# Attention tiles of the third and fourth unit: transposed in 32x32 blocks by VectorE and put in place through DRAM, in place of TensorE transposes

## The chip, the cores and the metric

The kernel runs on one core of a Trainium2 chip. The metric is the device time of one execution in microseconds, from repeated executions. A profiled execution leaves a trace, whose span goes from its first to its last instruction. Engines are named as in the profile: PE is TensorE's matmul, PEld its weight load, DVE VectorE, ACT ScalarE, POOL GpSimd and SP SyncE, whose queue issues nearly all DMAs. An L with a number is a line of the kernel.

## What is computed

Chunked attention (batch 8, 8 heads, 576 positions in chunks of 64, head dimension 64), and then a layer of three weight matrices with an elementwise maximum, and a projection:

```python
scores = scale * np.matmul(q_c, k_c.transpose(0, 1, 2, 4, 3))     # 64 x 64 for each chunk and head
scores = scores - np.max(scores, axis=-1, keepdims=True)
attn = np.exp(scores)
attn = attn / (np.sum(attn, axis=-1, keepdims=True) + 1e-09)
out = np.matmul(attn, v_c)
x = out of all heads side by side                                  # 4608 tokens x 512
h = np.maximum(np.maximum(x @ w1, x @ w2), x @ w3)                 # 512 -> 768
result = h @ w_out                                                 # 768 -> 512
```

All is float32. A product of the second part is made from three matmuls (`three`, L184 to L187) on a high and a low part of each operand.

## The kernel before

**Tiles, groups, units.** The 4608 tokens are 36 tiles of 128. Tiles 0 to 7 form the first group, written out by hand (`FIRST`), and a second group. The other 28 are worked in four units of 6, 8, 8 and 6 tiles (`UNITS`, L27). A unit has a hidden stage (9 sets of weights, `hidden`, L481, 14 steps of three matmuls in each set) and then a projection stage (`project`, L565, 6 steps of three matmuls for each tile, all on PE). The weights of a set come from DRAM into a ring of two buffers by two DMAs on SP's queue, of 768 KB (L465) and 1024 KB (L469). The load of set n + 2 is issued when set n is done (L778), and the load of a unit's last but one set takes the next unit's first set.

**Attention of a unit runs inside the hidden stage of the unit before it**, in pairs of tiles: `insertion` (L716) plans the steps of one pair. Pairs 0 to 2 are the first unit's, 3 to 6 the second's, 7 to 10 the third's and 11 to 13 the fourth's. For each tile of a pair: S (scores on PE, 32 small matmuls, L235), mx, sub, exp, sum, eps, rec (DVE and ACT), nrm (POOL, L202: the tile `e` is multiplied by 1 / sum), T (four PE transposes of 128x128 from `e` into PSUM, L258), at (ACT copies them into `xs`, L263), and V (32 small matmuls on PE, L274) in the *next* pair's insertion, with `xs` as the moving operand. V's results are copied into `stage` (L712), from which the next unit's operands are made (`operands`, L456) right behind the hidden stage.

**The order of the work** is fixed when the program is built. A clock `now` runs forward by `STEP_H` (0.6815 for a unit of 8 tiles) for each step of a set, and each planned piece of work has a due time on it. When a step passes it, the piece is emitted into its engine's queue, and `now` moves on by the PE time it is planned with: 0.65 for S, 0.5 for V, 0.46 for T, and nothing for others. All queues work in the order of emission. In a pair planned at `when`, V of the pair before and S come at `when`, and the other steps at `when` + 1 + the number in `PAIR` or `PAIR_T`, the first number for the pair's first tile, the second for its second. Insertions of a series stand at 9.0 behind the unit's start, and then evenly up to the length planned for the hidden stage less 3.5 (L737 to L744), so every 28.9 in the third unit's attention and every 41.6 in the fourth's. The last one of a series scores the next unit's first pair, and its T comes 14 later (`behind`).

**Room.** PSUM holds five banks for the hidden stage, taken in the order in which they came free (`take`, `give`); V takes two of them. Each of `raw`/`kk` (q and k), `vs` (v) and `e`/`et` has one buffer for the even and one for the odd tile; `xs` has two.

```python
def transposed():                                   # L261
    st["at"] = xs_p.tile([P, 4, P], F32, name="xs")
    nc.scalar.copy(out=st["at"], in_=st["tp"])
```

Of the kernel before, what the change touches and what calls it, by code (L numbers as in the profile page):

```python
# [9 lines left out]
F32 = mybir.dt.float32  # L10
# [10 lines left out]
P = 128  # L21
# [10 lines left out]
PAIR = (("mx", 1.4, 2.9), ("sub", 2.2, 3.7), ("exp", 3.1, 4.6), ("sum", 4.1, 6.0), ("eps", 5.0, 6.9), ("rec", 5.2, 7.1),  # L32
        ("nrm", 5.6, 7.5))
PAIR_T = (("T", 10.0, 12.4, 0.46), ("at", 10.9, 13.3, 0.0))
OPERANDS, SLOWER = (0.3, 2.0), (1.0, 1.8)
MIX = 0.5

# [26 lines left out]
def chunk_attn_maxout_kernel(  # L64
# [10 lines left out]
    nc = tc.nc  # L75
# [6 lines left out]
    xs_p = ctx.enter_context(tc.tile_pool(name="xs_p", bufs=2))  # L82
    ep = ctx.enter_context(tc.tile_pool(name="ep", bufs=1))
    ao_p = ctx.enter_context(tc.tile_pool(name="ao_p", bufs=1))
    stage_p = ctx.enter_context(tc.tile_pool(name="stage_p", bufs=1))
    dram = ctx.enter_context(tc.tile_pool(name="dram", bufs=1, space=bass.MemoryType.DRAM))
# [38 lines left out]
    for name in FIRST.split():  # L125
        k = (3 * int(name[1]) + int(name[2])) if name[0] in "WAXY" else None
# [62 lines left out]
    def over_sum(e):  # L189
        sm = tmp.tile([P, 32], F32, name="sm")[:, :8]  # L190

        def total():
            nc.vector.tensor_reduce(out=sm, in_=e, axis=AX.X, op=ALU.add)  # L193

        def guard():
            nc.vector.tensor_scalar_add(sm, sm, 1e-9)  # L196

        def invert():
            nc.vector.reciprocal(out=sm, in_=sm)  # L199

        def norm(eng=nc.gpsimd):
            eng.tensor_tensor(out=e, in0=e, in1=sm.unsqueeze(2).broadcast_to([P, 8, 64]), op=ALU.mult)  # L202

        return total, guard, invert, norm

    halves_of = [slice(0, 64), slice(64, 128)]
# [3 lines left out]
    def bank_of(name):  # L210
        if name not in banks_of:
            banks_of[name] = ps[name].tile([P, 2, 2, 4, 64], F32, name=name[-1])
        return banks_of[name]

    def plain_steps(t, x_of, col):


        st = {}

        def load_qk():  # L220
            st["r"] = att.tile([P, 2, 8, 64], F32, name="buf", tag=("raw", "kk", "aa")[t % 3] if t < 8 else ("raw", "kk")[t % 2],
                               bufs=1)
            nc.sync.dma_start(out=st["r"], in_=qk[t])

        def load_v():
            st["v"] = att.tile([P, 8, 64], F32, name="buf", tag=f"vs{t % 2}", bufs=1)
            nc.sync.dma_start(out=st["v"], in_=vb[t])

        def scores():
            r = st["r"]  # L230
            st["s"] = s = bank_of("ps_s")[:, :, t % 2 if t < 4 or "pair" in st else 0]
            for g in range(4):
                for h, c in quarters:
                    a, b = halves_of[c], halves_of[h]
                    nc.tensor.matmul(out=s[b, c, g, :], lhsT=r[a, 0, 2 * g + h, :], rhs=r[a, 1, 2 * g + h, :],  # L235
                                     start=True, stop=True)

        def maximum():
            st["mx"] = tmp.tile([P, 32], F32, name="mx")[:, :8]
            nc.vector.tensor_reduce(out=st["mx"].rearrange("p (g c) -> p c g", c=2), in_=st["s"], axis=AX.X, op=ALU.max)  # L240

        def less():
            st["e"] = ep.tile([P, 4, 2, 64], F32, name="e", tag=("et", "e")[t % 2])
            most = st["mx"].rearrange("p (g c) -> p c g", c=2)
            nc.vector.tensor_tensor(out=st["e"].rearrange("p g c k -> p c g k"), in0=st["s"],  # L245
                                    in1=most.unsqueeze(3).broadcast_to([P, 2, 4, 64]), op=ALU.subtract)

        def exp():
            nc.scalar.activation(out=st["e"], in_=st["e"], func=AF.Exp, scale=SCALE)

        def total():
            total, st["guard"], st["invert"], st["norm"] = over_sum(st["e"].rearrange("p g c k -> p (g c) k"))
            total()

        def transpose():
            st["tp"] = tp = ps_t.tile([P, 4, P], F32, name="tp")
            for g in range(4):
                nc.tensor.transpose(out=tp[:, g, :], in_=st["e"][:, g].rearrange("p c k -> p (c k)"),  # L258
                                    identity=ident)

        def transposed():  # L261
            st["at"] = xs_p.tile([P, 4, P], F32, name="xs")
            nc.scalar.copy(out=st["at"], in_=st["tp"])  # L263

        def values():
            if "pair" in st:
                x = [p[:, t % 2] for p in st["pair"]["x"]]
            else:
                st["x"] = bank_of("ps_x")[:, :, t % 2] if t < 4 else bank_of("ps_s")[:, :, 1]
                x = [st["x"][:, c] for c in range(2)]  # L270
            for g in range(4):
                for h, c in quarters:
                    a, b = halves_of[c], halves_of[h]
                    nc.tensor.matmul(out=x[c][b, g, :], lhsT=st["v"][a, 2 * g + h, :], rhs=st["at"][a, g, b],  # L274
                                     start=True, stop=True)

        def part(x):
            return x[:, :, col:col + P].rearrange("p g (c x) -> p c g x", c=2)

        def high():  # L280
            nc.scalar.copy(out=part(x_of()[0]), in_=st["x"])

        def low():
            xh, xl = x_of()
            nc.vector.tensor_tensor(out=part(xl), in0=st["x"], in1=part(xh).bitcast(F32), op=ALU.subtract)  # L285

        def pair(both):
            st["pair"] = both

        return dict(q=load_qk, v=load_v, pair=pair, S=scores, mx=maximum, sub=less, exp=exp, sum=total,  # L290
                    eps=lambda: st["guard"](), rec=lambda: st["invert"](), nrm=lambda *eng: st["norm"](*eng),
                    T=transpose, at=transposed, V=values, xh=high, xl=low)

    begun = {}

# [284 lines left out]
    def x_tiles(i):  # L580
        if i not in halves:
            halves[i] = [xp.tile([P, CT, 512], F32R, name=n, tag=f"{n}{i % 2}") for n in ("xh", "xl")]
        return halves[i]
# [22 lines left out]
    for t in range(8):  # L606
        ops.update((f"{n}{t}", fn) for n, fn in plain_steps(t, lambda i=t // 4: x_tiles(i), t % 4 * P).items())
# [57 lines left out]
    def plan(at, pe, fn):  # L665
        heapq.heappush(due, (at, len(order), pe, fn))
        order.append(fn)
# [20 lines left out]
    g = moe(starts[1], lambda: x_tiles(1))  # L688
# [5 lines left out]
    pairs = []  # L694
    for u, (_, t0, count) in enumerate(units):
        for n in range(0, count, 2):
            both = dict(col=n * P, norm=nc.gpsimd if u else nc.vector)
            both["tiles"] = [begun[t] if t in begun else plain_steps(t, stage, (t - t0) * P) for t in (t0 + n, t0 + n + 1)]
            for steps in both["tiles"]:
                steps["pair"](both)  # L700
            pairs.append(both)

    def value_banks(both):
        def fn():
            both["banks"] = [take() for _ in range(2)]
            both["x"] = [p.rearrange("p (s g x) -> p s g x", s=2, g=4) for p, _ in both["banks"]]
        return fn

    def staged(both, c):
        def fn():  # L710
            to = stage()[:, :, both["col"]:both["col"] + 2 * P].rearrange("p g (s c x) -> p c s g x", s=2, c=2)
            nc.scalar.copy(out=to[:, c], in_=both["x"][c])  # L712
            give(both["banks"][c][1])
        return fn

    def insertion(when, k, behind=0.0):  # L716

        scored = pairs[k]["tiles"] if k < len(pairs) else []
        if k:
            plan(when, 0.0, value_banks(pairs[k - 1]))  # L720
            for n, steps in enumerate(pairs[k - 1]["tiles"]):
                plan(when + 0.001 * (n + 1), 0.5, steps["V"])
                plan(when + 1.2 + 0.6 * n, 0.0, staged(pairs[k - 1], n))
        lead = 1.0 * bool(k)
        for n, steps in enumerate(scored):
            plan(when + 0.003 + 0.001 * n, 0.65, steps["S"])
            for name, *at in PAIR:
                fn = steps[name]
                plan(when + lead + at[n], 0.0, (lambda fn=fn: fn(pairs[k]["norm"])) if name == "nrm" else fn)
            for name, *at, pe in PAIR_T:  # L730
                plan(when + lead + behind + at[n], pe, steps[name])
            plan(when + 6.0 + n, 0.0, steps["v"])
        if k + 1 < len(pairs):
            for n, steps in enumerate(pairs[k + 1]["tiles"]):
                plan(when + 4.0 + n, 0.0, steps["q"])
# [99 lines left out]
```

## Time and profile before

| | us |
|---|---|
| median of 3 runs (lowest, highest) | 630.55 (630.23, 631.14) |
| the profiled execution | 631.41 |
| its span, first to last instruction | 629.6 |
| PE busy in it | 619.9 (98%) |
| PEld busy | 529.9 (84%) |
| DVE busy | 415.3 (66%) |
| ACT busy | 233.5 (37%) |
| POOL busy | 218.4 (35%) |
| mean granted TensorE clock | 0.999 of full speed |
| moved by DMA | 133.70 MB, 212 GB/s over the span |

Busy times of PE overlap with one another, as matmuls are pipelined, so 98% says that PE hardly ever stands still, and not how near it is to its peak. The chain of work that ended last gives each piece only the time by which it moves the end, and so tells what a piece on PE costs.

### The profile page before, as it was taken

The numbers are of one execution on the slowest core, as the hardware profiler recorded it, in microseconds if no ns is written. First come the engines' busy times: TensorE is split into PE (matmuls) and PEld (weight loads), VectorE is DVE, ScalarE is ACT, GpSimd is POOL, SyncE is SP. The second block draws the span as 40 slices with busy tenths as digits, with TensorE's granted clock in tenths as the row PEclk, the third lists the DMA queues.
The fourth block names the chain that finished last, engine by engine and source line by source line (L and its number), as shares of the span: only waits on it lengthen the run. The fifth ranks groups of instructions, "written<-read, shape, count | busy, mean of one in ns | idle before, by whom it ended". The sixth has DMA issues, their size and how long they took to land.

```text
span 629.6 us, 12374 instructions
## 1 busy us (share of the span) xinstructions
PE 619.9 (98%) x5102; PEld 529.9 (84%) x5102; DVE 415.3 (66%) x661; ACT 233.5 (37%) x400; POOL 218.4 (35%) x186
## 2 busy tenths in 40 slices
PE   7899999999999999999999999999999999999997
PEld 3788878887899999888888888888888888999986
DVE  4898965777949776956767679346585760366530
ACT  4897644444433242542323325222223141122121
POOL 2422576785413323424242325114141330222210
PEclk9999999999999999999999999999999999999999
DMA  8988658664958773825565717235545061366502
GB/s 329 353 306 264 239 184 326 259 238 162 366 190 299 283 285 140 332 102 218 194 260 184 268 56 312 84 126 226 217 168 209 32 279 67 135 241 256 205 18 83
DMA packets 36055, 133.70 MB, mean 212 GB/s; under 512 B 4000, under 2 KB 6560, under 8 KB 30240
## 3 DMA queue, kind: packets, MB, share of 16 engines
q1 hardware_dynamic: 35856, 132.79, 56.4%
q8 instruction: 40, 0.66, 0.4%
q10 hardware_dynamic: 144, 0.13, 0.1%
q14 instruction: 15, 0.12, 0.1%
HBM read 106.95 MB, written 25.95 MB: 211 GB/s over the span
## 4 chain that ended last, share of the span: by engine, by line
PE 92%; DVE 6%; ACT 1%; issue 1%; POOL 0%; DVEq 0%; ACTq 0%; POOLq 0%
PE pm L185 28%; PE pm L186 28%; PE pm L187 28%; PE s L235 2%; PE pm L274 2%; PE tp L258 2%; PE pm L627 1%; DVE e L245 1%; DVE s L406 1%; DVE sm L193 1%; DVE mx L240 1%; DVE sm L196 0%; POOL c L398 0%; DVE m L329 0%; DVE xl L285 0%
## 5 line engine op out<-in xcount | busy, mean ns | idle before, releaser
L185 PE MATMUL pm<-X,ring 128*128 128x512 f32 (+1 forms) x504 | 185.2, 368 | 0.1
L187 PE MATMUL pm<-X,ring 128*128 128x512 f32 (+1 forms) x504 | 182.5, 362 | 0.0
L186 PE MATMUL pm<-X,ring 128*128 128x512 f32 (+1 forms) x504 | 182.5, 362 | 0.0
L508 POOL TENSOR_TENSOR kept<-kept 128x384 f32<-128x384 f32 (+1 forms) x36 | 41.4, 1151 | 226.4 <-DVE kept L502 217.2
L502 DVE TENSOR_TENSOR kept<-pm,kept 128x384 f32<-128x384 f32 (+1 forms) x72 | 44.7, 621 | 98.4 <-PE pm L187 97.8
L185 PEld LDWEIGHTS pm<-X,ring 128*128 128x128 f32 x504 | 94.6, 188 | 10.7 <-DVE H L524 0.4
L187 PEld LDWEIGHTS pm<-X,ring 128*128 128x128 f32 x504 | 94.6, 188 | 10.1
L186 PEld LDWEIGHTS pm<-X,ring 128*128 128x128 f32 x504 | 94.7, 188 | 9.4
L499 ACT COPY kept<-pm 128x384 f32<-128x384 f32 (+1 forms) x72 | 38.4, 533 | 129.1 <-PE pm L187 124.6
L185 PE MATMUL pm<-woh,H 128*128 128x512 f32 x168 | 66.0, 393 | 0.0
L187 PE MATMUL pm<-woh,H 128*128 128x512 f32 x168 | 65.5, 390 | 0.0
L186 PE MATMUL pm<-wol,H 128*128 128x512 f32 x168 | 65.4, 390 | 0.0
L202 POOL TENSOR_TENSOR e<-e,sm 128x512 f32<-128x512 f32 x27 | 32.2, 1194 | 80.4 <-DVE sm L199 49.5
L185 PE MATMUL pm<-xh,wl 128*128 128x512 f32 (+1 forms) x156 | 60.1, 385 | 0.0
L186 PE MATMUL pm<-xl,wh 128*128 128x512 f32 (+1 forms) x156 | 58.4, 374 | 0.3 <-DVE xl L285 0.3
L187 PE MATMUL pm<-xh,wh 128*128 128x512 f32 (+1 forms) x156 | 58.3, 374 | 0.0
L505 DVE TENSOR_TENSOR pm<-pm,kept 128x384 f32<-128x384 f32 (+1 forms) x72 | 45.3, 629 | 14.8 <-PE pm L187 14.1
L514 DVE TENSOR_TENSOR most<-pm,most 128x384 f32<-128x384 f32 (+1 forms) x72 | 44.8, 622 | 2.1
L520 ACT CAST H<-most 128x384 fp32r<-128x384 f32 (+1 forms) x48 | 26.8, 570 | 43.0 <-DVE most L514 43.0
L240 DVE TENSOR_REDUCE mx<-s 128x8 f32<-128x512 f32 x36 | 24.6, 683 | 20.1 <-PE s L235 20.1
L187 PEld LDWEIGHTS pm<-woh,H 128*128 128x128 f32 x168 | 31.5, 188 | 6.6
L185 PEld LDWEIGHTS pm<-woh,H 128*128 128x128 f32 x168 | 31.5, 188 | 6.4
(93 smaller groups left out, 947.6 us busy)
## 6 DMA issues: line engine op xcount, KB each, us to landing
ring<-w SPq DMA_DIRECT2D x36, 1024.0 KB, 6.8
ring<-w SPq DMA_DIRECT2D x36, 768.0 KB, 4.5
buf<-in_qk SPq DMA_DIRECT2D x36, 512.0 KB, 6.2
buf<-in_vb SPq DMA_DIRECT2D x36, 256.0 KB, 6.5
w<-s SPq DMA_DIRECT2D x9, 1024.0 KB, 4.5
out_x<-ao SPq DMA_DIRECT2D x35, 256.0 KB, 2.0
stage<-in_w SPq DMA_DIRECT2D x7, 512.0 KB, 5.2
xl<-in_w SPq DMA_DIRECT2D x5, 512.0 KB, 8.2
```

The source lines that it names most:

```text
L185: nc.tensor.matmul(out=o, lhsT=al, rhs=bh, start=first, stop=False)
L186: nc.tensor.matmul(out=o, lhsT=ah, rhs=bl, start=False, stop=False)
L187: nc.tensor.matmul(out=o, lhsT=ah, rhs=bh, start=False, stop=last)
L202: eng.tensor_tensor(out=e, in0=e, in1=sm.unsqueeze(2).broadcast_to([P, 8, 64]), op=ALU.mult)
L235: nc.tensor.matmul(out=s[b, c, g, :], lhsT=r[a, 0, 2 * g + h, :], rhs=r[a, 1, 2 * g + h, :], start=True, stop=True)
L240: nc.vector.tensor_reduce(out=st["mx"].rearrange("p (g c) -> p c g", c=2), in_=st["s"], axis=AX.X, op=ALU.max)
L499: return lambda: nc.scalar.copy(out=kept(k), in_=o[i])
L502: return lambda: nc.vector.tensor_tensor(out=kept(k), in0=o[i], in1=kept(q), op=plus)
L505: return lambda: nc.vector.tensor_tensor(out=o[i] if w else M(j, c), in0=o[i], in1=kept(k), op=plus)
L508: nc.gpsimd.tensor_tensor(out=kept(2), in0=kept(2), in1=kept(1), op=plus)
L514: return lambda: nc.vector.tensor_tensor(out=M(j, c), in0=of(), in1=M(j, c), op=most)
L520: nc.scalar.copy(out=hh[j][:, c * half:(c + 1) * half], in_=M(j, c))
```

## The change

In the pairs of the third and fourth unit (pairs 7 to 13, 14 tiles; `u > 1`) T and at are replaced by three steps. `bt`: DVE transposes the tile's 32x32 blocks, in two instructions of 128x256, into a buffer of `xs`. `bw`: one DMA on SP's queue writes that tile (256 KB, in pieces of 1 KB) to DRAM. `br`: two DMAs on SP's queue read it back (128 KB each, in pieces of 512 bytes, 64 partitions each) into a new tile in the buffer of `e`, so that each block stands where the whole transpose would have it. V then takes its moving operand of 64 columns as two runs of 32. `now` is not moved forward for the new steps. Due times against `when`: bt at 9.6 and 11.5, bw at 10.6 and 12.5, br at 15.6 and 16.6 (T was at 11.0 and 13.4, at at 11.9 and 14.3).

```diff
--- before.py
+++ after.py
@@ -32,6 +32,7 @@
 PAIR = (("mx", 1.4, 2.9), ("sub", 2.2, 3.7), ("exp", 3.1, 4.6), ("sum", 4.1, 6.0), ("eps", 5.0, 6.9), ("rec", 5.2, 7.1),
         ("nrm", 5.6, 7.5))
 PAIR_T = (("T", 10.0, 12.4, 0.46), ("at", 10.9, 13.3, 0.0))
+PAIR_D = (("bt", 8.6, 10.5, 0.0), ("bw", 9.6, 11.5, 0.0), ("br", 14.6, 15.6, 0.0))
 OPERANDS, SLOWER = (0.3, 2.0), (1.0, 1.8)
 MIX = 0.5
 
@@ -262,6 +263,26 @@
             st["at"] = xs_p.tile([P, 4, P], F32, name="xs")
             nc.scalar.copy(out=st["at"], in_=st["tp"])
 
+        def blocks():
+            st["b"] = xs_p.tile([P, 4, 4, 32], F32, name="xs")
+            for c in range(2):
+                nc.vector.transpose(out=st["b"][:, 2 * c:2 * c + 2], in_=st["e"][:, :, c].rearrange("p g (k two) -> p two g k", two=2))
+
+        def to_scratch():
+            st["d"] = dram.tile([2, P, 2 * P], F32, name=f"b{t}")
+            nc.sync.dma_start(out=st["d"].rearrange("c p x -> p c x"), in_=st["b"].rearrange("p (c j) g x -> p c (j g x)", c=2))
+
+        def from_scratch():
+            st["at"] = ep.tile([P, 4, 4, 32], F32, name="e", tag=("et", "e")[t % 2])
+            for c, rows in enumerate(halves_of):
+                nc.sync.dma_start(out=st["at"][rows].rearrange("p i g x -> p i (g x)"),
+                                  in_=st["d"][c].rearrange("(i k) (j x) -> (k j) i x", i=4, j=2))
+
+        def moving(a, g, b):
+            if "d" in st:
+                return st["at"][a, b.start // 32:b.stop // 32, g, :]
+            return st["at"][a, g, b]
+
         def values():
             if "pair" in st:
                 x = [p[:, t % 2] for p in st["pair"]["x"]]
@@ -271,7 +292,7 @@
             for g in range(4):
                 for h, c in quarters:
                     a, b = halves_of[c], halves_of[h]
-                    nc.tensor.matmul(out=x[c][b, g, :], lhsT=st["v"][a, 2 * g + h, :], rhs=st["at"][a, g, b],
+                    nc.tensor.matmul(out=x[c][b, g, :], lhsT=st["v"][a, 2 * g + h, :], rhs=moving(a, g, b),
                                      start=True, stop=True)
 
         def part(x):
@@ -289,7 +310,7 @@
 
         return dict(q=load_qk, v=load_v, pair=pair, S=scores, mx=maximum, sub=less, exp=exp, sum=total,
                     eps=lambda: st["guard"](), rec=lambda: st["invert"](), nrm=lambda *eng: st["norm"](*eng),
-                    T=transpose, at=transposed, V=values, xh=high, xl=low)
+                    T=transpose, at=transposed, bt=blocks, bw=to_scratch, br=from_scratch, V=values, xh=high, xl=low)
 
     begun = {}
 
@@ -694,7 +715,7 @@
     pairs = []
     for u, (_, t0, count) in enumerate(units):
         for n in range(0, count, 2):
-            both = dict(col=n * P, norm=nc.gpsimd if u else nc.vector)
+            both = dict(col=n * P, norm=nc.gpsimd if u else nc.vector, turn=PAIR_D if u > 1 else PAIR_T)
             both["tiles"] = [begun[t] if t in begun else plain_steps(t, stage, (t - t0) * P) for t in (t0 + n, t0 + n + 1)]
             for steps in both["tiles"]:
                 steps["pair"](both)
@@ -727,7 +748,7 @@
             for name, *at in PAIR:
                 fn = steps[name]
                 plan(when + lead + at[n], 0.0, (lambda fn=fn: fn(pairs[k]["norm"])) if name == "nrm" else fn)
-            for name, *at, pe in PAIR_T:
+            for name, *at, pe in pairs[k]["turn"]:
                 plan(when + lead + behind + at[n], pe, steps[name])
             plan(when + 6.0 + n, 0.0, steps["v"])
         if k + 1 < len(pairs):
```

## Rows read from the trace of the kernel before

**Rows 1.** The page, busy time, share of the span and instructions by engine.

```profile
PE 619.9 (98%) x5102; PEld 529.9 (84%) x5102; DVE 415.3 (66%) x661; ACT 233.5 (37%) x400; POOL 218.4 (35%) x186
```

**Rows 2.** Waits of PE, whole span: who waited for whom, us, times, longest.

```profile
PE tp L258 <- POOL e L202: 1.9, 2, 1.2
PE pm L627 <- DVE h L629: 1.2, 1, 1.2
```

**Rows 3.** Chain that ended last, around one pair's transposes: start us, us, what.

```profile
298.27 0.23 PE pm L187
298.50 0.44 PE tp L258 x4
298.94 0.23 PE pm L185
```

**Rows 4.** The same chain: first and last transposes of pairs 7 to 13.

```profile
275.59 0.44 PE tp L258 x4
...
474.30 0.44 PE tp L258 x4
```

**Rows 5.** Groups by line, 270 to 480 us: engine, op, shapes, count | busy, mean ns | idle.

```profile
L258 PE MATMUL tp<-ident,e 128*128 128x128 f32 x56 | 8.4, 272 | 0.0
L263 ACT COPY xs<-tp 128x512 f32<-128x512 f32 x14 | 8.2, 588 | 22.8 <-PE tp L258 22.8
```

**Rows 6.** Groups by line, whole span: the nearest DVE work, and the smallest.

```profile
L561 DVE COPY ao<-pm 128x256 f32<-128x256 f32 x1 | 0.4, 425 | 21.4 <-ACT ao L560 21.4
L199 DVE RECIPROCAL sm<-sm 128x8 f32<-128x8 f32 x36 | 7.2, 201 | 1.0
```

**Rows 7.** DVE in order of time, where pair 8's bt would stand [idle before <-releaser].

```profile
297.17 0.70 DVE L505 TENSOR_TENSOR pm<-pm,kept 128x512 f32<-128x512 f32 x1 [0.60 <-PE pm L187]
...
299.34 0.69 DVE L514 TENSOR_TENSOR most<-pm,most 128x512 f32<-128x512 f32 x1
300.37 0.70 DVE L505 TENSOR_TENSOR pm<-pm,kept 128x512 f32<-128x512 f32 x1 [0.33 <-PE pm L187]
...
301.71 0.68 DVE L514 TENSOR_TENSOR most<-kept,most 128x512 f32<-128x512 f32 x1
303.66 0.69 DVE L502 TENSOR_TENSOR kept<-pm,kept 128x512 f32<-128x512 f32 x1 [1.27 <-PE pm L187]
```

**Rows 8.** Busy time by stretch there: us, then PE, PEld, DVE, ACT, POOL, clock, DMA, GB/s.

```profile
290.00:300.00 10.00, 10.00 (x54) 8.26 (x47) 8.98 (x16) 3.21 (x6) 4.63 (x4) 1.00 0.79 319
300.00:310.00 10.00, 10.00 (x48) 8.24 (x47) 5.65 (x10) 2.38 (x4) 2.59 (x2) 1.00 0.47 184
```

**Rows 9.** POOL in order of time: the second nrm of pair 8.

```profile
296.07 1.04 POOL L202 TENSOR_TENSOR e<-e,sm 128x512 f32<-128x512 f32 x1 [0.43 <-DVE sm L199]
```

**Rows 10.** SP's queue in order of time: issues of ring loads in the second unit.

```profile
300.36 0.33 SPq L465 DMA_DIRECT2D ring<-w  x1
...
310.39 0.32 SPq L465 DMA_DIRECT2D ring<-w  x1
...
353.97 0.33 SPq L465 DMA_DIRECT2D ring<-w  x1
...
373.99 0.32 SPq L465 DMA_DIRECT2D ring<-w  x1
```

**Rows 11.** The 1024 KB load issued at 300.73 (L469): its landing.

```profile
DMA to landing us min/median/max: 6.3/6.3/6.3
```

**Rows 12.** The page, DMA issues: engine, op, count, KB each, median us to landing.

```profile
out_x<-ao SPq DMA_DIRECT2D x35, 256.0 KB, 2.0
w<-wh SPq DMA_DIRECT2D x9, 256.0 KB, 4.3
w<-wh SPq DMA_DIRECT2D x9, 128.0 KB, 4.1
```

**Rows 13.** The chain of rows 3: V of pairs 7 and 8 (64 matmuls, two tiles).

```profile
288.08 1.09 PE pm L274 x64
...
316.48 1.09 PE pm L274 x64
```

## Prediction, made before the changed kernel was run

> **What bounds the kernel now.** First the busy times: PE is busy for 98% of the span and every other engine, its own weight loads aside, for at most 66% [rows 1]. That alone proves little, as PE's times overlap, so the second view is what PE waits for: the longest entry is 1.9 us in two waits, for POOL's nrm ahead of a transpose, and the next is at the very start [rows 2]. Asked for 265 to 480 us alone, where the changed pairs are, the list is empty. So PE is never kept waiting there, and any work taken off its queue shortens the run by what that work costs in the queue. The third view, the chain of work that ended last, gives this cost.
>
> **The change part by part.**
>
> *Four transposes of a tile leave PE.* A transpose is shown as 0.27 us long, and 56 of them as 8.4 us busy [rows 5], but neither is the cost, since their fill overlaps with the neighbours. In the chain the four of one tile take 0.44 us, and the matmuls on either side keep their pitch of 0.23 [rows 3]. Fourteen such pieces stand in the chain from 275.59 to 474.30 us [rows 4]: 14 x 0.44 = 6.2 us. As PE waits for nothing there, the whole of it is on the path. By the Trainium skill (VectorE: DVE Perf Modes, section The three transpose paths) a 128x128 transpose on TensorE is 390 ns, which as an estimate would make the gain 56 x 0.39 = 21.8 us. The row decides: pipelined between matmuls, one costs 0.11 us.
>
> *Fourteen copies of 0.59 us leave ACT* [rows 5], 8.2 us. ACT is busy for 37% and waits for PE ahead of them; nothing waits for it. Worth 0.
>
> *Two bt for a tile on DVE, 28 in all.* No row shows a block transpose. The nearest is a DVE copy of 128x256 float32, 0.425 us; from below the fixed part of a small instruction, 0.20 us [rows 6]; from above, four passes over the tile, an estimate of 4 x 0.425 = 1.7 us. I take the nearest, 0.43, as an instruction over 256 columns. So a pair adds 4 x 0.43 = 1.7 us (0.8 to 6.8) in two portions of 0.9 us, 2 us apart. None of it is on PE's queue; what hides it is DVE's idle time and the slack of the banks. Pair 8's bt would stand among the instructions from 297.17 on: there DVE is busy for 8.98 of 10 us, and then for 5.65 of 10 [rows 8], so a lag of up to 4.35 us is made good by about 310. What is behind a bt on DVE is the reading of PSUM banks. The last of a set's readings ends near 301.8 (the piece ahead of the one at 301.71) [rows 7], 1.5 us after its set, which ended when the ring load at 300.36 went out [rows 10]. With five banks and 6 x 0.23 = 1.4 us for each, the bank is wanted again four banks later, 5.5 us after its end. That leaves 4.0 us, and the bt take 1.7 of it. Cost 0 at up to 4.0 / 4 = 1.0 us for one bt; above that, PE stalls. bt doesn't wait for nrm: pair 8's second one ends at 297.1 [rows 9], and its bt is due 11.5 behind `when`, where V ran at 288.08 [rows 13]: near 299.6. The last operand work (L454) of the next unit is due 18.9 behind the hidden stage, ahead of the bt of pairs 7 and 11, and DVE is then free.
>
> *One bw and two br for a tile on SP's queue, 42 DMAs.* SP spends about 0.4 us on an issue [rows 10], and mostly waits. The DMAs add 14 x 0.5 = 7 MB to 133.7. What has to be seen is who stands behind a waiting DMA. bw waits for bt, and br for the landing of bw, about 2 us when the queue is empty (256 KB: 2.0 us) [rows 12]. Behind them on SP are the ring loads, and only these can reach PE.
> Due times show where they meet, counted from the unit's start. Pair 8 (and pair 12): `when` = 9.0, second bw due 21.5; set 2 begins at 2 x 14 x 0.6815 + 2.3 (V and S) = 21.4, and its ring load is due at 21.7, right behind the bw. There bt would push the DVE work of 297.17 to 301.7 by 0.9 us ahead of the second bt and end near 301.6 [rows 7], so the load leaves SP near 302.0 or a bit later and not at 300.36: 1.7 us late, and 0.3 for bw's issue. Its data stand behind 256 KB, 0.8 us by rate: 1.75 MB of ring landed 6.7 us after the first issue [rows 10, 11], 256 KB in 2.0, so 1.5 MB take 4.7. The 1024 KB land at 300.73 + 6.3 = 307.0 before; then 2.0 + 0.8 later, near 309.8. Set 3 begins at 310.4 [rows 10], less 0.9 for the two transposes gone, and wants these weights from its second accumulation on, 1.4 later: 310.9. So 1.1 us is left. Cost 0; with the four bt at 0.7 us and more it is a stall of some tenths.
> Pair 9: bw due 0.1 and 2.0 ahead of a load, none delayed. Pair 13: first bw 0.9 ahead of a load, the second just behind it, so that it lands with the ring some 7 us later, and its br holds SP until shortly before the next load. Pair 10: second br due at 66.7 + 16.6 = 83.3, and the load of the next unit's first set at 8 x 14 x 0.6815 + 6.9 + 0.3 = 83.5. That load holds SP for a whole set, as before (353.97, then 373.99) [rows 10]. The br just gets ahead of it. Pairs 7 and 11 have no ring load near.
> V wants the tile 28.4 us after V of the pair before [rows 13]; br goes out at 16.6 and lands some 2 to 7 us later, which leaves 5 us. In pair 7 the last br goes out near 281 and V comes at 287: 3 us left. Cost 0.
> The pieces of 512 bytes have no row; pieces of 1 KB land like those of 2 KB (4.1 us for 128 KB, 4.3 for 256 KB) [rows 12], so I take them at the common rate, and up to twice its time. The Trainium skill warns against moving a transpose into plain DMAs (VectorE: DVE Perf Modes, section The three transpose paths: a copy that rearranges by strides is 19 times slower than the hardware's own transpose). It has a place among the rivals.
>
> *Moved by the clock.* Without T's 0.46 the sets end earlier on `now`, and the last insertion of the third unit's series, due at 95.6, comes 2.8 behind the hidden stage (92.8) and not at its end; the fourth's 1.8 behind. On PE it is the same work in another order. `stage` is filled by 4.6 and read at 4.9 (L457); DVE may wait some tenths, and the projection (33 us) covers that. Of the five banks the projection has two by then, V two, and one is left for its third tile. Cost 0.
>
> *V's moving operand in two runs of 32.* No row has such an operand. Between 0 and twice V's time (14 x 0.545 = 7.6 us); I take 0, since the same number of columns is streamed.
>
> **Sum.** 631.41 - 6.2 = 625.2 us for the profiled execution. It lies 0.86 above the median of 630.55, so the median should come out at 624.4.
>
> **The rivals.**
> (1) *Ring loads come late* behind a bw that waits for bt. For: 1.1 us left in pairs 8 and 12. Against: PE waits for no load now. With bt at 0.85 us, twice my figure, the second bt ends 1.3 us later and the load likewise: 0.2 us at two places; with the 512-byte pieces slow as well, or DVE's order less kind, 1 to 2 us at two or three places: up to 4 us, 625 to 628.5.
> (2) *DVE becomes the bound, slower than before.* If a bt takes four passes (1.7 us), a pair adds 6.8 us where the banks allow 4.0: 2.8 us stall in pairs 8, 9, 10, 12 and 13, or 14 us, 638. It decides from a stall of 1.24 us in each, a bt of (4.0 + 1.24) / 4 = 1.3 us. Against: every DVE row of 256 columns is at 0.42 or so.
> (3) *The reads hold the DMA engines, slower.* A pair reads 512 KB, 1.6 us by rate. From one ring load to the next are 9.5 us, of which the ring takes 6.7 [rows 10, 11], so 2.8 are free; and its last part is wanted 9.5 + 1.4 behind its issue, which leaves 4.2 of slack. From reads of 7.0 us on PE stalls, from 8.2 (five times the rate) in pairs 8, 9, 10, 12 and 13 the gain is gone, and at six times (9.6) it is 5 x 2.6 = 13 us, 637.5. Against: each piece is contiguous on both sides. By the Trainium skill's 19 times (the section named above) it would be 30 us a pair and some 740, as an estimate; no row shows such a copy.
> (4) *V takes longer* with two runs: at twice the time 624.4 + 7.6 = 632.0.
> (5) That the transposes aren't on the path, 630.5: PE's empty list of waits speaks against it.
>
> **How the numbers follow.** Forecast (623.7 to 625.2) 0.68; (1) 0.17; (2) 0.04; (3) 0.03; (4) 0.04, of which half ends within 0.2%; (5) 0.04. The range leaves the last four out (0.15): low 623.6, as a piece may cost 0.45 and a run vary by 0.4, high 628.0. This kernel's runs can tell 0.2% (1.3 us) from no change. Faster: 0.68 + 0.17 + 0.01 = 0.86; same: 0.02 + 0.04 = 0.06; slower 0.08.
>
> **What would show it.** L258 leaves the chain after 265 us and keeps 22 of 36 pieces; V's pieces stay at 1.09 for a pair; PE's list of waits stays as short as it is. A bt row near 0.43 us. A PE entry that waits for the ring's DMA is rival 1 or 3, one behind DVE readings of pm rival 2, V at over 1.09 rival 4. Wrong too if PE waits for br ahead of V.

## The result

The changed kernel takes 624.14 us (median of 4 runs, 622.97 to 624.42), the kernel before beside it 630.44 us (630.23 to 631.14). The ratio is 0.9895, with a 95% interval of 0.9877 to 0.9912: 6.6 us less, 5.5 to 7.8; the two medians differ by 6.3. The forecast was 624.4 us in a range of 623.6 to 628.0. The profiled execution took 623.88 us, its span 622.1.

In the changed kernel later lines have moved: T is L259, bt L269, bw L273, br L278, V L295, the ring loads L486 and L490, the three matmuls L186 to L188. The page of the profile after, busy times and the lines' shares of the chain that ended last:

```profile
PE 612.0 (98%) x5045; PEld 524.2 (84%) x5046; DVE 422.5 (68%) x689; ACT 226.1 (36%) x386; POOL 217.4 (35%) x186
PE pm L186 28%; PE pm L187 27%; PE pm L188 27%; PE s L236 2%; PE pm L295 2%; DMA ring<-w 1%; PE tp L259 1%; DVE e L246 1%; DVE s L427 1%; PE pm L648 1%; DVE sm L194 1%; DVE mx L241 1%; DVE sm L197 0%; POOL c L419 0%; DVE m L350 0%
```

Against [rows 1], PE is busy 7.9 us less, ACT 7.4 us less and DVE 7.2 us more. T, which is still done in the unchanged pairs, keeps 1% of the chain. The longest of PE's waits over the whole span (who for whom, us, times, longest):

```profile
PE tp L259 <- POOL e L203: 1.9, 2, 1.2
PE pm L648 <- DVE h L650: 1.2, 1, 1.2
PE s L236 <- DVE e L246: 0.7, 2, 0.6
PE pm L186 <- DMA ring<-w: 0.7, 1, 0.7
...
```

One of them is new, 0.7 us for a ring load near 200 us; it lies in the second unit's attention, which is not changed, and the first run below, which has none of the new steps, has it too (0.8 us). Between 265 and 500 us, where all changed pairs are, the list is as empty as it was before. The chain, where [rows 4] had fourteen pieces of 0.44 us, now has only V and S of a pair between the matmuls (here pairs 7 and 8, where [rows 13] had the same 1.09 us for V):

```profile
241.52 0.44 PE tp L259 x4
...
286.28 1.09 PE pm L295 x64
287.37 0.93 PE s L236 x64
...
315.05 1.09 PE pm L295 x64
```

The new steps, first as the groups of DVE's work and of DMA issues (engine, size, median us to landing), then pair 8's, DVE and SP in order of time:

```profile
L269 DVE STREAM_TRANSPOSE xs<-e 128x256 f32<-128x256 f32 x28 | 10.4, 413 | 0.0
```
```profile
b<-xs SPq DMA_DIRECT2D x14, 256.0 KB, 2.8
e<-b SPq DMA_DIRECT2D x28, 128.0 KB, 4.5
```
```profile
294.08 0.69 DVE L523 TENSOR_TENSOR kept<-pm,kept 128x512 f32<-128x512 f32 x1
294.69 0.76 DVE L269 STREAM_TRANSPOSE xs<-e 128x256 f32<-128x256 f32 x2
295.38 0.70 DVE L526 TENSOR_TENSOR pm<-pm,kept 128x512 f32<-128x512 f32 x1
...
297.41 0.76 DVE L269 STREAM_TRANSPOSE xs<-e 128x256 f32<-128x256 f32 x2
...
300.00 0.68 DVE L535 TENSOR_TENSOR most<-kept,most 128x512 f32<-128x512 f32 x1
300.88 0.69 DVE L523 TENSOR_TENSOR kept<-pm,kept 128x512 f32<-128x512 f32 x1 [0.20 <-PE pm L188]
```
```profile
295.48 3.10 SPq L273 DMA_DIRECT2D b<-xs  x2
298.67 0.42 SPq L486 DMA_DIRECT2D ring<-w  x1
299.14 0.45 SPq L490 DMA_DIRECT2D ring<-w  x1
299.69 2.77 SPq L278 DMA_DIRECT2D e<-b  x4
```

DVE works without a gap from the first bt to 300.7, where [rows 7] had gaps of 0.60 and 0.33 us; by 300.88 it has caught up. The second bw goes out at 298.2 and the ring load follows it at 298.67.

### The profile page after: what moved, and what is told of

Read it like the earlier page. It is cut to its first block, busy times and chain, and to the rows that moved or that the text cites. A ratio compares the mean times of both kernels' runs of the same rounds, so it can differ in the third digit from the quotient of the medians.

```text
span 622.1 us, 12385 instructions
## 1 busy us (share of the span) xinstructions
PE 612.0 (98%) x5045; PEld 524.2 (84%) x5046; DVE 422.5 (68%) x689; ACT 226.1 (36%) x386; POOL 217.4 (35%) x186
## 4 chain that ended last, share of the span: by engine, by line
PE 90%; DVE 6%; DMA 1%; ACT 1%; issue 1%; POOL 0%; SPq 0%; DVEq 0%; ACTq 0%; POOLq 0%
PE pm L186 28%; PE pm L187 27%; PE pm L188 27%; PE s L236 2%; PE pm L295 2%; DMA ring<-w 1%; PE tp L259 1%; DVE e L246 1%; DVE s L427 1%; PE pm L648 1%; DVE sm L194 1%; DVE mx L241 1%; DVE sm L197 0%; POOL c L419 0%; DVE m L350 0%
## 5 line engine op out<-in xcount | busy, mean ns | idle before, releaser
L186 PE MATMUL pm<-X,ring 128*128 128x512 f32 (+1 forms) x504 | 184.2, 365 | 0.7 <-DMA ring<-w 0.7
L188 PE MATMUL pm<-X,ring 128*128 128x512 f32 (+1 forms) x504 | 182.4, 362 | 0.0
L186 PEld LDWEIGHTS pm<-X,ring 128*128 128x128 f32 x504 | 94.6, 188 | 11.7 <-DVE most L535 1.0
L188 PEld LDWEIGHTS pm<-X,ring 128*128 128x128 f32 x504 | 94.6, 188 | 9.9
L186 PE MATMUL pm<-woh,H 128*128 128x512 f32 x168 | 65.6, 390 | 0.0
L188 PE MATMUL pm<-woh,H 128*128 128x512 f32 x168 | 65.4, 389 | 0.0
L186 PE MATMUL pm<-xh,wl 128*128 128x512 f32 (+1 forms) x156 | 60.1, 385 | 0.0
L188 PE MATMUL pm<-xh,wh 128*128 128x512 f32 (+1 forms) x156 | 58.3, 374 | 0.0
L186 PEld LDWEIGHTS pm<-woh,H 128*128 128x128 f32 x168 | 31.5, 188 | 6.6
L188 PEld LDWEIGHTS pm<-woh,H 128*128 128x128 f32 x168 | 31.5, 188 | 6.5
```

The costliest lines, as they stand in the source:

```text
L186: nc.tensor.matmul(out=o, lhsT=al, rhs=bh, start=first, stop=False)
L188: nc.tensor.matmul(out=o, lhsT=ah, rhs=bh, start=False, stop=last)
```

## Experiments

Each stands beside runs of the kernel before on the same chip (medians 630.93, 630.59 and 630.27 us in the three series). Edits are against the changed kernel, but for that of the planner's clock alone.

**Nothing in place of the transposes.**

```diff
-PAIR_D = (("bt", 8.6, 10.5, 0.0), ("bw", 9.6, 11.5, 0.0), ("br", 14.6, 15.6, 0.0))
+PAIR_D = (("br", 14.6, 15.6, 0.0),)
         def from_scratch():
-            st["at"] = ep.tile(...)           # and the two reads, cut here
+            st["at"] = st["e"]...              # seen as [P, 4, 4, 32]
```

> The four transposes and the copy of pairs 7 to 13 are taken away and nothing takes their place: no bt, no bw, no br, V reads the untransposed tile (so attention of these tiles is not what it should be). Theory: the replacement costs PE nothing, all of the change's gain is the 14 x 0.44 us off PE's queue; the time is that of the changed kernel, 624.1 us within 0.5, ratio to before 0.989 to 0.991. Rival (the replacement has a hidden price on DVE, SP or the DMA engines, and the transposes were worth more than 6.2 us): 1 us or more below, 623 or less.

Measured: 623.71 us (623.21 to 625.17), ratio 0.9900, 0.9882 to 0.9917. The whole replacement costs nothing that can be measured: there are 0.4 us between the medians, inside either interval, and these are about 1 us wide to either side.

**Both ways at once.**

```diff
-PAIR_D = (("bt", 8.6, 10.5, 0.0), ...
+PAIR_D = (("T", 10.0, 12.4, 0.46), ("tc", 10.9, 13.3, 0.0), ("bt", 8.6, 10.5, 0.0), ...
+        def copied():
+            aside = xs_p.tile([P, 4, P], F32, name="ys", bufs=1)
+            nc.scalar.copy(out=aside, in_=st["tp"])
```

> The changed kernel, with T and its copy by ACT back in pairs 7 to 13 (the copy into a buffer that nothing reads) beside bt, bw and br. Theory (the gain is the transposes alone, and all new steps are hidden): the time of the kernel before, 630.4 us within 0.6. Rival (something else in the change brings or takes time): off from that by 1 us or more.

Measured: 631.17 us (629.64 to 632.29), ratio 1.0012, 1.0001 to 1.0022. With the transposes back the time of before is back, although all new steps are there too: 0.6 us above it, 0.1 to 1.4 by the interval. Together the two runs show it from both sides: the gain goes and comes with the transposes and their copy by ACT, and everything else in the change counts for no more than about 1 us. The copy has no run of its own; that it is worth nothing rests on the chain, in which no piece of ACT stands between 265 and 500 us before.

They show one more thing. The spans of the changed kernel and of before differ by 7.5 us, and from V of pair 6 (249.49, before 250.35) to the end by 6.7, where 6.2 were reckoned. Measured as the mean distance between the starts of neighbouring matmuls of the hidden stages from 270 to 520 us, the pitch is 0.2274 us before (724 of them), 0.2275 with both ways (724), and 0.2268 in the changed kernel and in the run with nothing in place (744 each). In the kernel before the pitch is 0.2300 within eight instructions of a transpose (110 of the 724) and 0.2270 elsewhere. So the transposes also slow the matmuls near them; over 744 matmuls the 0.0006 are 0.5 us, and they make up the difference.

**The planner's clock alone**, in the kernel before:

```diff
+PAIR_T0 = (("T", 10.0, 12.4, 0.0), ("at", 10.9, 13.3, 0.0))     # for the third and fourth unit
```

> The kernel before, with T of pairs 7 to 13 planned at 0 and not at 0.46 of the planner's clock, so that insertions stand against the sets as in the changed kernel; no work is added or taken away. Theory (the move is free): 630.4 us within 0.5. Rival (the last insertion of a unit, now in the projection, was worth something by itself): off by 1 us or more either way.

Measured: 630.24 us (629.31 to 631.46), ratio 0.9994, 0.9985 to 1.0004. The move is free, as far as the interval tells (0.9 us less to 0.3 more).

**Each bt twice, and four times.**

```diff
-            for c in range(2):
+            for c in [0, 1] * 2:        # the other: * 4
                 nc.vector.transpose(...)
```

> Each block transpose of the changed kernel is issued twice, so a tile's bt take 1.65 us of DVE and not 0.83 (a pair 3.3). Theory (DVE's lag is hidden by the banks up to about 4.0 us a pair): no change, 624.1 us, at most 0.5 more where the ring load behind the second bw leaves SP later in pairs 8 and 12. Rival (DVE is already at its limit in the stretch of a bt): the added 1.65 us a pair show in five pairs, 8 us more, 632.

Measured: 624.02 us (622.32 to 624.99), ratio 0.9895, 0.9874 to 0.9916. No change: twice the DVE work is hidden too. (Four bt in a row hold DVE for 1.41 us, so a pair's take 2.8 us and not 3.3.)

> Each block transpose is issued four times: 6.6 us of DVE a pair. Theory (4.0 us of slack in the banks, then PE stalls): 2.6 us a pair in the five pairs 8, 9, 10, 12 and 13, 13 us in all, 637, with PE waiting behind DVE readings of pm; part of it is also waiting for ring weights in pairs 8 and 12, whose load stands behind a bw that waits for bt. Rival (the slack is much larger than reckoned, DVE makes it good within the period of 28 us): below 628.

Measured: 631.04 us (629.94 to 633.43), ratio 1.0008, 0.9996 to 1.0021. That is 6.9 us more than the changed kernel, between theory (13) and rival (below 4); PE's waits account for 5.3 of it. PE's waits from 265 to 500 us, and the chain at pairs 8 and 12:

```profile
PE pm L186 <- DMA ring<-w: 2.7, 2, 1.9
PE pm L186 <- DVE most L535: 2.6, 3, 1.7
```
```profile
299.69 2.64 DVE xs L269 x8
303.29 7.40 DMA ring<-w
...
428.80 2.64 DVE xs L269 x8
432.39 8.57 DMA ring<-w
...
474.12 2.05 DVE xs L269 x7
```

Both mechanisms are there and at the pairs named: in 8 and 12 the ring load stands behind a bw that waits for bt (0.8 and 1.9 us of PE), in 8, 12 and 13 PE waits for a bank that DVE has yet to read (0.5, 0.5, 1.7). Pairs 9 and 10 don't stall at all, though DVE has the same work there. So the reckoning that every pair over 4.0 us pays the rest doesn't hold. The added work, too, is less than was expected: eight bt in a row hold DVE for 2.72 us and not for 8 x 0.413 = 3.3, so a pair's take 5.4 us and not 6.6. By the same reckoning that would be 1.4 us in each of five pairs, 7.0; that 6.9 were measured is luck, as two of the five paid nothing. Why these two have room is not shown: in pair 9, too, DVE has no gap from its first bt (325.56) until 337.4.

**One br behind the ring loads.**

```diff
-("br", 14.6, 15.6, 0.0))
+("br", 14.6, 16.6, 0.0))
```

> One number: the second tile's br is due 1.0 later, 15.6 becomes 16.6. In pair 10 alone this puts it behind the two ring loads of the next unit's first set, which hold SP's queue until the last set of the unit is done; elsewhere the order of the queue is the same. Theory (the margin of 0.2 on the planner's clock is what keeps this pair free): the read goes out near 370 us and not at 362.5, lands behind 1.75 MB near 376, and V of that tile, wanted near 373.1, waits about 3 us; total 627 us, one wait of PE for the DMA into e. Rival (V isn't that near, or the read overtakes the ring's data): no change, 624.1.

Measured: 631.08 us (629.05 to 632.95), ratio 1.0009, 0.9995 to 1.0022. One due time, later by 1.0, changes the order of SP's queue in this one pair and takes back the whole gain. PE's one wait between 265 and 500 us, and the chain there:

```profile
PE pm L295 <- DMA e<-b: 4.6, 1, 4.6
```
```profile
370.05 0.58 SPq L278
...
370.68 7.38 DMA e<-b
...
378.10 0.96 PE pm L295 x27
...
379.17 1.71 PE s L236 x63
```

The mechanism is as expected, the price twice as high. The read, issued at 370.68 behind 1.75 MB, lands 7.4 us later and V waits 4.6 us, not 3. Another 2 us go behind the wait: S takes 1.71 us and not 0.93. The view by stretch (us, PE, PEld, DVE, ACT, POOL busy, granted clock, DMA, GB/s) says why:

```profile
374.00:376.00 2.00, 0.00 (x0) 0.00 (x0) 0.62 (x2) 0.00 (x0) 0.00 (x0) 1.00 1.00 387
376.00:378.00 2.00, 0.29 (x2) 0.19 (x2) 0.00 (x0) 0.00 (x0) 0.00 (x0) 1.00 1.10 332
378.00:379.00 1.00, 0.90 (x36) 0.91 (x40) 0.00 (x0) 0.00 (x0) 0.00 (x0) 0.60 1.05 438
379.00:380.00 1.00, 1.00 (x48) 1.00 (x44) 0.00 (x0) 0.81 (x2) 0.00 (x0) 0.50 1.01 426
380.00:381.00 1.00, 1.00 (x34) 0.88 (x28) 0.70 (x1) 0.27 (x1) 0.00 (x0) 0.50 0.89 377
381.00:382.00 1.00, 1.00 (x4) 0.82 (x5) 1.00 (x2) 0.39 (x1) 0.39 (x1) 0.69 0.87 176
382.00:383.00 1.00, 1.00 (x6) 0.82 (x5) 0.96 (x3) 0.78 (x2) 1.00 (x1) 1.00 0.96 332
```

After standing still for the wait, PE is granted 0.50 of full speed (1.2 of 2.4 GHz) from shortly behind 378 until shortly before 382; the 0.60 and 0.69 belong to stretches in which it changes.

**Each br four times.**

```diff
-            for c, rows in enumerate(halves_of):
+            for c, rows in list(enumerate(halves_of)) * 4:
```

> Each br is issued four times: a pair reads 2 MB and SP issues 16 reads, 0.6 us each in the changed kernel's trace, 9.6 us of SP's queue. Theory (2.8 us free between ring loads and 4.2 us of slack): reads of 1.9 x 4 = 7.6 us are just over 7.0, so 0 to 3 us more, 624 to 627, with PE waiting for ring weights; SP's queue alone holds a ring load back by some 1.3 us, which the slack takes. Rival (the engines or the queue are fuller than reckoned): 10 us more, 634 or above.

Measured: 710.21 us (706.14 to 712.53), ratio 1.1256, 1.1210 to 1.1303. Far beyond both, but it didn't measure what it was meant to. The repeated reads write the same tile, so each waits for the landing of the one before it into the same half. SP's waits of that kind, 73 of them, and below them what PE waited for most:

```profile
SPq L278 <- DMA e<-b: 74.9, 73, 6.3
```
```profile
PE pm L295 <- DMA e<-b: 41.0, 14, 7.8
PE pm L186 <- DMA ring<-w: 21.4, 2, 11.1
...
```

SP is held by the reads for 18 to 24 us in each pair, and ring loads and the tile itself come late. What it shows is the price of a held SP queue, not of the reads. Their rate is better seen in the changed kernel itself: on an empty queue (pair 10, 361 to 364 us) four reads of 128 KB go out some 0.65 us apart and land 2.5 to 2.9 us after their issue. What the reads alone cost the DMA engines has no run of its own.

**Each bw four times**, the added ones to DRAM tiles of their own:

```diff
+            for n in range(3):
+                aside = dram.tile([2, P, 2 * P], F32, name=f"b{t}x{n}")
+                nc.sync.dma_start(out=aside.rearrange(...), in_=st["b"].rearrange(...))
```

> Each bw of the changed kernel is issued four times, the added three to DRAM that nobody reads: 1.5 MB more of writes for a pair. In pairs 8 and 12 the second tile's three stand ahead of the ring load and put 3 x 0.38 us of issue and 0.75 MB, 2.4 us by rate, before it. In the changed kernel these loads land 2.5 and 1.6 us before PE wants them. Theory: they come 1 to 2 us late, PE waits for ring weights at these two places, in all 2 to 4 us, and each stop costs some more for a lower clock behind it: 626 to 630. In the other pairs nothing. Rival A (the engines take it in passing): 624.1. Rival B (br waits longer for the landing of a bw in a queue of four, and V comes late): waits of V for e, 632 or more.

Measured: 628.75 us (626.81 to 633.13), ratio 0.9976, 0.9954 to 0.9999. Of PE's waits in its profiled execution (627.04 us) only these are for the ring:

```profile
PE pm L186 <- DMA ring<-w: 2.3, 3, 1.2
...
```

The size is as expected and V waits for nothing, but of the places only pair 8 is right (0.6 us); the other waits are in pair 9 (1.2) and pair 13 (0.5), and pair 12 has none. In 9 and 13 added writes now stand close ahead of the load: in pair 9 its second DMA lands 10.0 us after its issue and not 7.1 as in the changed kernel, in pair 13 9.2 and not 7.1. It needs 1.5 MB more for a pair to get there. A lower clock behind the stops is not seen in this execution: none of these waits is over 1.2 us, and the mean clock is 1.000. The two longest of the ten executions (632.41 and 633.13 us) have 0.997, and no trace shows where they stopped.

**The second unit too, and then its first pair alone.**

```diff
-turn=PAIR_D if u > 1 else PAIR_T
+turn=PAIR_D if u > 0 else PAIR_T
```

> One sign: pairs of the second unit (3 to 6, 8 tiles) get the new steps too. Their transposes are 8 x 0.44 = 3.5 us of the chain. Theory (the gain is the transposes' place on PE as long as no wait comes up): 624.1 - 3.5 = 620.6 us, less what the ring of the first unit's stage loses: there a set lasts 7.2 us and not 9.5, a ring load 6.7, so the slack is 1.6 us and not 4.2, and the changed kernel's profile already has one wait of PE for ring weights there, of 0.7 us. Expected 620.6 to 622.5, with a wait or two for the ring near 190 to 250 us. Rival (any tile moved costs as much in the tighter stage as it brings): 624 or more.

Measured: 643.95 us (642.2 to 645.61), ratio 1.0212, 1.0190 to 1.0234: 13 us slower than before. PE's waits, and a piece of the chain with pair 5:

```profile
PE pm L295 <- DMA e<-b: 5.0, 4, 2.2
PE pm L295 <- issue: 5.0, 1, 5.0
PE pm L186 <- DMA ring<-w: 4.6, 4, 1.6
...
```
```profile
225.18 0.69 DVE xs L269 x2
225.88 5.38 DMA b<-xs
...
231.31 0.58 SPq L278
...
233.31 5.43 DMA e<-b
238.87 0.85 PE pm L295 x29
```

The waits for the ring are what was feared (4.6 us), but twice as much is V waiting for its tile (the 5.0 listed under "issue" end at 267.76, when the first read of that tile has just landed, at 267.67). In pairs 4 to 6 a bw in a queue full of ring loads lands 5 to 7 us after its issue, br waits for that and lands 3 to 7 us after its own, and here V comes some 21 us behind S and not 29. With the mean clock at 0.989 (1.1% of 640 us, 7 us) for the stops, 14.6 + 7 us of the 23 us missing against 620.6 are found.

The first pair of that unit alone, with an offset of its own on the due times:

```diff
+            both["early"] = -6.0 * (u == 1 and n == 0)      # added to the due times; and PAIR_D for this pair
```

> Of the second unit only its first pair (3) gets the new steps, 6 earlier on the planner's clock than pairs 7 and 11 have theirs, so that they lie in the second group's projection, where no ring load is due for them to meet. Theory (what cost the second unit its gain was a bw whose landing waits behind ring loads in sets of 7.2 us, and a br that waits for it): no such wait here, and two tiles more gain 2 x 0.44 = 0.9 us: 623.2 us, 622.8 to 624.2. Rival (the stretch ahead of the first unit is too full of DMAs as well): a wait of V, 626 or more.

Measured: 623.81 us (622.08 to 625.27), ratio 0.9894, 0.9877 to 0.9912. No wait of V, so the rival falls; but that it is 0.9 us faster than the changed kernel can't be told from these runs. No version clearly beat the changed kernel.

## Why the prediction was right, point by point

*Where PE stands, and what a transpose costs there.* Right. Fourteen pieces of 0.44 us left the chain, and with the pitch of the matmuls nearby, which had not been reckoned with, the profile lost 6.7 us from the changed stretch on where 6.2 were reckoned. The medians differ by 6.3; that this comes within 0.1 of the sum is luck, as the interval goes from 5.5 to 7.8. The two runs that take away and give back T and its copy put the 56 transposes at 7.2 and 7.0 us between medians (630.93 - 623.71 and 631.17 - 624.14), 0.13 us each with the slowing of their neighbours, and the chain at 0.11. As an estimate, the 390 ns of the Trainium skill (VectorE: DVE Perf Modes, section The three transpose paths), which the page states for bf16, would have made it 21.8 us; the runs decide against it as a price in the queue.

*bt.* 0.413 us measured, 0.43 taken. (Not every DVE row of 256 columns is at 0.42, as rival 2 has it: a memset, L629, takes 0.27. Nothing hangs on it.) That it costs nothing is shown by the run with twice as many. The reckoned limit (4.0 us of DVE for a pair) lies between the run with 2.8 us, which shows no stall, and the one with 5.4, which does. The price above the limit, by which rival 2 came to 14 us, is not borne out: it charges all five pairs, and two of them didn't stall.

*bw and the ring load behind it.* Right in the result, with the step off in size. The first bt went out ahead of the L505 of [rows 7] and not behind, at 294.69; so the load behind the second bw left 12.4 us behind V (298.67 - 286.28) against 12.3 before (300.36 [rows 10] - 288.08 [rows 13]), and not 1.7 late. Its 1024 KB landed 7.2 us after its issue, 0.9 more than before [rows 11] with 0.8 reckoned, near 306.35; that is 2.5 us ahead of PE's need (the set starts at 307.5, and wants them 1.4 later) where 1.1 had been reckoned. In pair 12, where the landing took 8.2 us, it was 1.6. In pair 9 the prediction has bw 0.1 and 2.0 ahead of a load; they left 4.7 and 2.7 us ahead of it (324.20, 326.22, then 328.90), and the cost of 0 holds all the more.

*br.* An issue costs SP 0.6 us and not the 0.4 taken from the ring's rows. That the reads cost nothing here is shown by the run with nothing in place, which is not faster by more than can be told (0.4 us); what rival 3 would have cost, no run settled. The 19 times of the Trainium skill (VectorE: DVE Perf Modes, section The three transpose paths) are stated for a large stride in the innermost dimension of the destination. These pieces are contiguous on both sides, and nothing like it shows: 128 KB landed in 2.5 to 2.9 us on an empty queue. The least room ahead of V was in pair 7, as reckoned: its last read landed at 282.5, V began at 286.21.

*Pair 10.* The margin of 0.2 on the planner's clock is real, and it is the most valuable number of the prediction: crossing it costs 7 us. It is a margin of order and not of time: in the changed kernel the pair's four reads left from 361.23 on and the load behind them, which waits for its set, at 369.23. It was given no price and no place among the rivals, and it should have had both. Likewise V's wait for br had one line at the end; on a tighter stage it is the largest cost (the second unit).

*Moved by the clock, V in two runs.* Both free, as taken: 0.9994 for the clock, and 1.09 us for a pair's V before and after.

## What to carry to other kernels

Where one engine never waits, the chain of work tells what a piece in its queue is worth, and neither its shown duration nor its busy time does; a detour by other engines and DRAM is then paid for only by margins. List those margins before the change, each with what stands behind it in an in-order queue: a detour that writes, waits and reads has a latency that depends on whatever else is in the queue (here 2 to 8 us for each leg). And price a missed margin at more than the wait, since PE can come back from a stop at a lower clock: behind the wait of 4.6 us it did, while in the run with each bt four times the granted clock stayed at 1.00 from 270 to 490 us, in spite of waits of up to 1.9 us.

## What the runs showed of the hardware that was not expected

- Transposes slow the matmuls around them: a pitch of 0.2300 us within eight instructions of one, 0.2270 elsewhere, and 0.2268 in the kernel without them.
- The shown times of block transposes that follow one another on DVE overlap: one of 128x256 float32 is shown as 0.413 us, but two in a row take 0.76, four 1.41 and eight 2.72, so each after the first adds 0.33.
- A stop of PE of 4.6 us cost 6.7 us of span: behind it the granted clock was 0.50 for some 3 us.
- In the changed kernel a DMA of 128 KB in pieces of 512 bytes takes SP 0.60 us to issue (median of 28, 0.57 to 0.84), a ring load of 1024 KB 0.43 (median of 36). On an empty queue the former lands 2.5 to 2.9 us after its issue.
